# Placing the stages of a linear attention one by one between the MLP parts of the same kernel

## The chip, the cores and the metric

The kernel runs on one core of a Trainium2 chip. Such a core has engines that each work through their own list of instructions in order: TensorE (PE in the profile: matrix products, which read SBUF and write PSUM; its weight loads are shown as PEld), VectorE (DVE), ScalarE (ACT), GpSimd (POOL) and SyncE (SP, which here only issues DMAs). They wait for each other through semaphores. The metric is the time of one execution on the device in microseconds; the lower the better.

## The reference

The reference is a gated linear attention followed by an MLP with a residual.

```python
f = 1.0 / (1.0 + np.exp(-f_logit))              # (4, 8, 768, 48), as q, k and v
for t in range(S):
    state = f[:, :, t, :, None] * state + np.einsum('bhd,bhe->bhde', k[:, :, t], v[:, :, t])
    y[:, :, t] = np.einsum('bhd,bhde->bhe', q[:, :, t], state)
...
x = y.transpose(0, 2, 1, 3).reshape(4, 768, 384)
xn = (x - mu) / np.sqrt(var + 1e-06) * g_ln     # mean and variance of each row of 384
out = x + np.maximum(xn @ w_ch1, 0.0) @ w_ch2   # 384 x 1536 and 1536 x 384
```

The inputs of the attention are float32. The weights w_ch1 and w_ch2 arrive as 64-bit floating point numbers, and the kernel turns them into float32 on the chip.

## The kernel before, in words

**Units.** The sequence is cut into twelve units of 64 steps. A unit holds these 64 steps of all four batches and eight heads, that is 256 rows for the MLP, in two groups g of 128 rows. Only a state of 48 x 48 for each batch and head goes from one unit to the next.

**The attention of a unit** (attention(n), lines 494 to 624) is a generator with four stages, each ended by a yield:

1. TensorE transposes f (line 505), ScalarE makes the gates with a sigmoid (533), and VectorE runs two scans along the time: after (518), the product of the gates from a step to the end of the unit, and upto (527), the other way round, started from the reciprocal of the whole product (523, 525). least (538) keeps the smallest whole product, for a check at the end.
2. k and q are transposed, and VectorE multiplies them with the scans into kh and qh (546).
3. VectorE decays the state into kept (553). TensorE multiplies qh with kept into py (563) and kh with qh into the scores ps (573). VectorE masks them (576). kh is transposed back (584) and copied by ScalarE (586).
4. TensorE adds the scores times v to py (593). ScalarE copies py to x (604). VectorE takes the statistics of x (606, 607), GpSimd makes the reciprocal standard deviation (608, 609). TensorE forms the new part of the state (616), VectorE adds it (621; in unit 0 it copies it, 623).

Then normalize(n) (631, VectorE) and turn(n) (641 on TensorE, 643 on ScalarE) give xt, the operand of the MLP.

**The MLP of a unit** (mlp(n), lines 647 to 671) is a generator with twelve parts. Parts 0 to 5 form the first product, 256 of the 1536 columns each (656: twelve matmuls, as each float32 product is two instructions), with a ReLU on ScalarE (658). Parts 6 to 11 form the second product for the two groups (663, eight matmuls each). After parts 8 and 11 VectorE adds x (668), and SP writes the rows out (670).

**The weights.** w1 and w2 are cut into six pieces each (pieces, 428 to 433). A piece of w1 is what one of the parts 0 to 5 reads; a piece of w2 serves two steps of a group's sum of twelve. fetch() issues the DMA of a piece's words. split() (450 to 470) takes exponent and mantissa apart on VectorE (461, 463), converts both on ScalarE (465, 466), and lets GpSimd clamp and shift the exponent (468). join() (472 to 481) puts mantissa, sign and exponent together on VectorE (477, 479, 481).

**The order** is written by hand: each engine gets its instructions in the order in which the program emits them. After the first two units' attention and MLPs, whose order carries the weight conversion along (675 to 706), the loop of line 719 runs MLP m part by part, and between the parts the attention of unit m + 1: stage 1 after part 0, stage 2 after part 1, stage 3 after part 5, stage 4 after part 7, normalize after part 9, turn after part 10, and the loads of unit m + 2 after part 2. Unit 2's attention lies in the loop of line 709, between the second products of units 0 and 1.

**Buffers.** PSUM has eight banks. Four single banks (ps1, one_bank) serve, in turn, the transposes, parts 0 to 5, and one per group of the second product; two pairs of banks (ps2, two_banks) serve py, ps and the state. The transposed k and q take two single banks each, until kh and qh are formed. f, k and q have two buffers in SBUF, v three, the words of the weights three, and their exponents and mantissas two each.

Of the kernel before, what the change touches and what calls it, by code (L numbers as in the profile page):

```python
# [303 lines left out]
def kernel(  # L304
# [21 lines left out]
    P = 128  # L326
# [51 lines left out]
    def load(n, engines):  # L378
        if n >= NU:
            return  # L380
        vt = raws.tile([P, G, H, D], FP32, tag="rawv", name=f"v{n}")
        tiles = [wide_heads[name, n % 2] for name in "fkq"] + [vt]
        loaded[n] = tiles
        for t, src in zip(tiles, (f_logit, k, q, v), strict=True):
            for b in range(B):
                engines[b % len(engines)].dma_start(
                    out=t[(b % 2) * T:(b % 2 + 1) * T, b // 2, :, 0:D],
                    in_=src[b, :, n * T:(n + 1) * T, :].rearrange("h p d -> p h d"))

    load(0, (nc.sync, nc.scalar))  # L390
# [10 lines left out]
    power = consts.tile([P, 2], FP32)  # L401
    nc.vector.memset(power, -0.5)
    bias = consts.tile([P, 1], FP32)
    nc.vector.memset(bias, float(-BIAS))

    warm = consts.tile([P, 1], FP32)
    nc.scalar.activation(out=warm, in_=power[:, 0:1], func=AF.Sigmoid)
# [15 lines left out]

    load(1, (nc.sync,))
    nc.sync.dma_start(out=gain, in_=moe_g_ln.rearrange("(c p) -> p c", p=P))
# [24 lines left out]
    def split():  # L450

        if not fetched:
            return
        name, words, to, r, w = fetched.pop(0)
        scale = stage.tile([P, r, w], I32, tag="scale", bufs=2, name=f"{name}scale")
        frac = stage.tile([P, r, w], FP32, tag="frac", bufs=2, name=f"{name}frac")
        wv = words.rearrange("p r (f two) -> p two r f", two=2)
        low, high = wv[:, 0].bitcast(U32), wv[:, 1]


        nc.vector.tensor_scalar(out=scale, in0=high, scalar1=20, scalar2=0x7FF,
                                op0=ALU.logical_shift_right, op1=ALU.bitwise_and)
        nc.vector.tensor_scalar(out=frac.bitcast(I32), in0=high, scalar1=0xFFFFF, scalar2=None,
                                op0=ALU.bitwise_and)
        nc.scalar.activation(out=scale, in_=scale, func=AF.Relu, bias=bias, scale=1.0)  # L465
        nc.scalar.activation(out=frac, in_=frac.bitcast(I32), func=AF.Copy, bias=1.0,
                             scale=2.0 ** -20)
        nc.gpsimd.tensor_scalar(out=scale, in0=scale, scalar1=255.0, scalar2=float(1 << 23),  # L468
                                op0=ALU.min, op1=ALU.mult)
        opened.append((low, high, scale, frac, to))  # L470
# [23 lines left out]
    def attention(n):  # L494

        fr, kr, qr, vt = loaded.pop(n)
# [17 lines left out]
        def scans(s0, s1):  # L514
            c0, c1 = s0 * E1, s1 * E1
            flat = "p s e -> p (s e)"

            nc.vector.tensor_tensor_scan(  # L518
                out=after.rearrange(flat)[:, c0:c1][:, ::-1],
                data0=gt[:, c0 + 1:c1 + 1][:, ::-1],  # L520
                data1=ends.rearrange(flat)[:, c0:c1][:, ::-1], initial=0.0,
                op0=ALU.mult, op1=ALU.add)
            nc.vector.tensor_scalar_max(out=total[:, s0:s1], in0=after[:, s0:s1, 0],
                                        scalar1=1e-30)
            nc.vector.reciprocal(out=st[:, s0:s1, 0], in_=total[:, s0:s1])

            nc.vector.tensor_tensor_scan(  # L527
                out=upto.rearrange(flat)[:, c0:c1], data0=gt[:, c0:c1],
                data1=st.rearrange(flat)[:, c0:c1], initial=0.0, op0=ALU.mult, op1=ALU.add)

        for g in range(G):
            pt = across(fr, g)
            nc.scalar.activation(out=gv[:, g * HS:(g + 1) * HS, 1:E1], in_=pt, func=AF.Sigmoid)  # L533
            if n == 0:
                scans(g * HS, (g + 1) * HS)
# [12 lines left out]
        yield  # L548


        if n:
            kept = work.tile([P, 2, GA, D], FP32, tag="kept", name=f"kept{n}")
            nc.vector.tensor_tensor(
                out=kept, in0=state, op=ALU.mult,
                in1=total.rearrange("p (e b) -> p b e", b=2).unsqueeze(3).broadcast_to(
                    [P, 2, GA, D]))

# [11 lines left out]
        for e in range(GA):  # L569
            for b in range(2):  # L570
                for r in range(2):
                    seg = 2 * e + b
                    nc.tensor.matmul(ps[half(b), r, e], lhsT=kh[head_rows(r), seg],  # L573
                                     rhs=qh[head_rows(r), seg], start=True, stop=True)
        sc = work.tile([P, 2, GA, T], FP32, tag="sc", name=f"sc{n}")
        nc.vector.tensor_tensor(  # L576
            out=sc.rearrange("s r e t -> s (r e) t"), in0=ps.rearrange("s r e t -> s (r e) t"),
            in1=causal.unsqueeze(1).broadcast_to([P, 2 * GA, T]), op=ALU.mult)
        kt = work.tile([P, GA, P], FP32, tag="kt", name=f"kt{n}")
# [7 lines left out]
        yield  # L587
# [15 lines left out]
        for g in range(G):  # L603
            nc.scalar.copy(out=x[:, g].rearrange("t (a r d) -> t r a d", r=2, d=D),  # L604
                           in_=pyv[:, g])
            nc.vector.bn_stats(out=stats[:, g], in_=x[:, g])  # L606
# [3 lines left out]
        norm_of[n] = mv, rstd  # L610
        if n < NU - 1:
# [10 lines left out]
            else:  # L622
                nc.vector.tensor_copy(out=state, in_=pnv)
        yield
# [48 lines left out]


    for _ in range(3):
        fetch()
    first, second = attention(0), attention(1)
    for stages in (first, first, first, second, first, second):
        next(stages)
    normalize(0)  # L680
    turn(0)
    split()
    next(second)
    split()
    join()
    fetch()
    mlps = mlp(0), None
    for part in range(6):
        next(mlps[0])
        if part == 0:  # L690
            next(second)
        elif part == 1:
            normalize(1)
        elif part == 2:
            turn(1)
        split()
        join()
        fetch()
    mlps = mlps[0], mlp(1)
    for part in range(6):  # L700
        next(mlps[1])
        split()
        join()
        fetch()
        if part == 3:
            load(2, (nc.sync,))
    assert not (queue or fetched or opened)
    third = attention(2)
    for part in range(12):
        next(mlps[part // 6])  # L710
        if part in (1, 2, 5, 7):
            next(third)
        elif part == 3:
            load(3, (nc.sync,))
        elif part == 9:
            normalize(2)
        elif part == 10:
            turn(2)
    for m in range(2, NU):
        n = m + 1  # L720
        stages = attention(n) if n < NU else iter(())
        parts = mlp(m)
        for slot in range(12):
            next(parts)
            if slot in (0, 1, 5, 7):
                next(stages, None)
            elif slot == 2:
                load(n + 1, (nc.sync,))
            elif slot == 9 and n < NU:
                normalize(n)  # L730
            elif slot == 10 and n < NU:
                turn(n)
            if n == NU and slot == 2:
# [46 lines left out]
```

## Time and profile before

| what | value |
| --- | --- |
| time, median of three runs | 586.15 us (585.65 to 586.56) |
| time of the profiled execution | 586.91 us |
| its span, from the first to the last instruction | 585.2 us |
| mean granted TensorE clock | 0.947 of full speed |
| TensorE busy | 518.4 us (89%) |
| VectorE busy | 217.5 us (37%) |
| ScalarE busy | 118.4 us (20%) |
| GpSimd busy | 52.9 us (9%) |

The profile shows one execution. Busy times are sums of an engine's instructions. A group of instructions is given as line, engine, operation, output <- inputs, shapes, count, busy time, mean ns of one, and the idle time just before it with what ended it. In a row of the timeline the first number is the start in us and the second the length. In a row of the chain it is the same, without the engine's waits. A row of the windows gives the stretch, its length, then the busy time and the number of instructions of TensorE, its weight loads, VectorE, ScalarE and GpSimd, then the granted clock, the share of the DMA engines, and GB/s.

### The profile page before, as it was taken

To read this page: it belongs to the slowest core of one execution; us is meant where nothing else is said; L and a number is where in the kernel's file an instruction comes from. 1 tells how busy PE (TensorE), PEld (TensorE's weight loads), DVE (VectorE), ACT (ScalarE), POOL (GpSimd) and SP (SyncE) were. 2 spreads that over 40 slices of the span, in tenths; PEclk is the share of its full clock that TensorE was granted. 3 is DMA by queue.
4 is the path that set the end of the run, shared out by engine and by line. 5 is a ranking of instruction groups with operands and counts; after the bars stand their busy time and mean duration, and the time that the engine had idled before them with its cause. 6 is when DMAs were issued, how large, how long until landed. Compare 5 with 4: busy or idle time off the path is not lost.

```text
span 585.2 us, 10892 instructions
## 1 busy us (share of the span) xinstructions
PE 518.4 (89%) x4841; PEld 396.7 (68%) x4841; DVE 217.5 (37%) x312; ACT 118.4 (20%) x242; POOL 52.9 (9%) x53
## 2 busy tenths in 40 slices
PE   4645779789899899989989989989989989989996
PEld 3644558456686686777777777777777777777773
DVE  4774878922412323323232233232232242252000
ACT  1242435200211211211211211211211211211110
POOL 3024448200000000000000000000000000000000
PEclk9957779989989989989989999989989989999999
DMA  9901535760420320330330330330340240100101
GB/s 141 232 7 55 162 115 168 95 136 16 76 47 15 73 50 10 72 56 2 69 67 2 62 73 3 70 65 3 60 76 2 52 85 2 28 0 2 27 4 31
DMA packets 109703, 33.83 MB, mean 58 GB/s; under 512 B 102736, under 2 KB 105808, under 8 KB 109648
## 3 DMA queue, kind: packets, MB, share of 16 engines
q1 hardware_dynamic: 105424, 32.26, 26.8%
q10 hardware_dynamic: 4224, 0.79, 1.1%
q8 instruction: 40, 0.66, 0.5%
q14 instruction: 15, 0.12, 0.1%
HBM read 28.31 MB, written 4.72 MB: 56 GB/s over the span
## 4 chain that ended last, share of the span: by engine, by line
PE 72%; DVE 19%; ACT 3%; issue 1%; POOL 1%; DMA 1%; DVEq 0%; ACTq 0%
PE po L663 31%; PE ph L656 28%; DVE upto L527 5%; DVE after L518 5%; PE py L593 4%; PE ps L573 2%; PE py L563 2%; PE kp L584 2%; ACT gates L533 2%; DVE w L481 2%; PE pn L616 2%; PE xp L641 1%; DVE kh L546 1%; DVE w_0scale L479 1%; DMA qraw<-in_q_dram 1%
## 5 line engine op out<-in xcount | busy, mean ns | idle before, releaser
L656 PE MATMUL ph<-xt,w 128*128 128x256 f32 x864 | 213.2, 408 | 38.0 <-DVE kh L546 21.1
L656 PEld LDWEIGHTS ph<-xt,w 128*128 128x128 f32 x864 | 176.1, 206 | 70.8 <-DVE kh L546 23.2
L663 PE MATMUL po<-w,h 128*128 128x384 f32 x576 | 194.5, 492 | 0.6 <-DVE w L481 0.6
L663 PEld LDWEIGHTS po<-w,h 128*128 128x128 f32 x576 | 107.7, 191 | 70.0 <-issue 1.5
L658 ACT ACTIVATE h<-ph 128x512 f32<-128x512 f32 x72 | 42.9, 597 | 215.1 <-PE ph L656 215.1
L576 DVE TENSOR_TENSOR sc<-ps,causal 128x1024 f32<-128x1024 f32 x12 | 14.7, 1225 | 110.4 <-PE ps L573 110.4
L668 DVE TENSOR_TENSOR o<-x,po 128x384 f32<-128x384 f32 x24 | 13.3, 554 | 109.9 <-PE po L663 109.9
L608 POOL TENSOR_SCALAR rstd<-mv 128x2 f32<-128x2 f32 x12 | 2.7, 223 | 455.3 <-DVE mv L607 455.3
L606 DVE BATCH_NORM_STATS2 stats<-x 128x6 f32<-128x384 f32 x24 | 13.0, 543 | 81.8 <-ACT x L604 81.8
L518 DVE TENSOR_TENSOR_SCAN after<-gates,ends 128x1040 f32<-128x1040 f32 (+1 forms) x13 | 28.0, 2156 | 41.0 <-ACT gates L533 41.0
L643 ACT ACTIVATE xt<-xp,gain 128x128 f32<-128x128 f32 x72 | 19.9, 376 | 91.6 <-PE xp L641 91.6
L527 DVE TENSOR_TENSOR_SCAN upto<-gates,starts 128x1040 f32<-128x1040 f32 (+1 forms) x13 | 28.1, 2158 | 0.4
L593 PEld LDWEIGHTS py<-v,sc 64*64 64x64 f32 x768 | 23.3, 135 | 5.9 <-issue 5.9
L593 PE MATMUL py<-v,sc 64*64 64x48 f32 x768 | 24.8, 219 | 0.0
L604 ACT COPY x<-py 128x384 f32<-128x384 f32 x24 | 10.3, 482 | 67.5 <-PE py L593 67.5
L586 ACT COPY kt<-kp 128x512 f32<-128x512 f32 x24 | 13.1, 588 | 53.7 <-PE kp L584 53.7
L468 POOL TENSOR_SCALAR w_0scale<-w_0scale 128x768 int32<-128x768 int32 x7 | 22.2, 3171 | 14.7 <-ACT w_0scale L465 14.7
L573 PE MATMUL ps<-qh,kh 48*64 48x64 f32 x768 | 15.2, 235 | 5.7 <-DVE qh L546 5.7
L573 PEld LDWEIGHTS ps<-qh,kh 48*64 48x64 f32 x768 | 14.0, 149 | 6.2 <-DVE qh L546 6.2
L505 PE MATMUL tr<-ident,fraw 128*128 128x128 f32 x96 | 13.6, 285 | 5.1 <-DMA fraw<-in_f_logit_dram 5.1
L505 PE MATMUL tr<-ident,qraw 128*128 128x128 f32 x96 | 13.6, 286 | 3.6 <-DVE o L668 2.8
L505 PEld LDWEIGHTS tr<-ident,fraw 128*128 128x128 f32 x96 | 11.8, 148 | 6.7 <-POOL causal L398 4.4
(95 smaller groups left out, 328.8 us busy)
## 6 DMA issues: line engine op xcount, KB each, us to landing
w_0words<-in_moe_w_ch_dram SPq DMA_DIRECT2D x7, 768.0 KB, 4.3
out_dram<-o SPq DMA_DIRECT2D x48, 96.0 KB, 2.2
fraw<-in_f_logit_dram SPq DMA_DIRECT2D x46, 96.0 KB, 3.0
kraw<-in_k_dram SPq DMA_DIRECT2D x46, 96.0 KB, 3.2
qraw<-in_q_dram SPq DMA_DIRECT2D x46, 96.0 KB, 3.0
v<-in_v_dram SPq DMA_DIRECT2D x46, 96.0 KB, 3.2
w_256words<-in_moe_w_ch_dram SPq DMA_DIRECT2D x1, 768.0 KB, 6.2
w_512words<-in_moe_w_ch_dram SPq DMA_DIRECT2D x1, 768.0 KB, 8.7
```

What stands on the lines that cost most here:

```text
L468: nc.gpsimd.tensor_scalar(out=scale, in0=scale, scalar1=255.0, scalar2=float(1 << 23), op0=ALU.min, op1=ALU.mult)
L505: nc.tensor.transpose(pt[:, a * P:(a + 1) * P], src[:, g, 2 * a:2 * a + 2].rearrange("p h e -> p (h e)"), ident)
L518: nc.vector.tensor_tensor_scan(out=after.rearrange(flat)[:, c0:c1][:, ::-1], data0=gt[:, c0 + 1:c1 + 1][:, ::-1], data1=ends.rearrange(fla ...
L527: nc.vector.tensor_tensor_scan(out=upto.rearrange(flat)[:, c0:c1], data0=gt[:, c0:c1], data1=st.rearrange(flat)[:, c0:c1], initial=0.0, op ...
L573: nc.tensor.matmul(ps[half(b), r, e], lhsT=kh[head_rows(r), seg], rhs=qh[head_rows(r), seg], start=True, stop=True)
L576: nc.vector.tensor_tensor(out=sc.rearrange("s r e t -> s (r e) t"), in0=ps.rearrange("s r e t -> s (r e) t"), in1=causal.unsqueeze(1).broa ...
L593: nc.tensor.matmul(py[half(b), r, e * D:(e + 1) * D], lhsT=sc[half(b), r, e], rhs=vt[half(b), g, 2 * a + r], start=n == 0 and e == 0, stop ...
L643: nc.scalar.mul(out=xt[:, m, g * P:(g + 1) * P], in_=pt[:, m], mul=gain[:, m:m + 1])
L656: nc.tensor.matmul(ph[:, j], lhsT=w1[:, m, (i + j) * P:(i + j + 1) * P], rhs=xt[:, m], start=m == 0, stop=m == KD - 1)
L658: nc.scalar.activation(out=h[:, i:i + 2], in_=ph, func=AF.Relu)
L663: nc.tensor.matmul(po, lhsT=h[:, i, g * P:(g + 1) * P], rhs=w2[:, i], start=i == 0, stop=i == KF - 1)
L668: nc.vector.tensor_tensor(out=o, in0=x[:, g], in1=po, op=ALU.add)
```

## The change

The generator of the attention now has named stages: gates, after, upto, k, q, scores, causal, kt, values, stats, state, norm and turn follow one another (norm and turn, the former normalize and turn, are called from it), and each place names the stages that it runs. In the loop over the later units, gates and after follow part 0, upto part 1, k part 2, q (with least and kept) part 3, scores, causal and kt part 5, values, stats and state part 7, norm part 9, turn part 10; the loads go from behind part 2 to behind part 3. Unit 2's attention is spread likewise.

In the first two units w1 is converted between unit 0's stages and the first parts of its MLP, before unit 1's scans; w2's pieces come in unit 1's attention and in the first parts of its MLP. join() comes ahead of split() of the next piece. The loads of unit 0 leave ScalarE's queue except two of f, the first two weight pieces are fetched ahead of unit 1's loads, and ScalarE's first sigmoid comes before k, q and v are issued. GpSimd's clamp and shift becomes two instructions on ScalarE, and unit 0's state is copied by ScalarE.

```diff
-    def load(n, engines):
+    def load(n, name, engines=(nc.sync,)):
...
-    load(0, (nc.sync, nc.scalar))
+    load(0, "f", (nc.sync, nc.scalar))
+
+    power = consts.tile([P, 2], FP32)
+    nc.vector.memset(power, -0.5)
+    warm = consts.tile([P, 1], FP32)
+    nc.scalar.activation(out=warm, in_=power[:, 0:1], func=AF.Sigmoid)
+    for name in "kqv":
+        load(0, name)
...
+    full = consts.tile([P, 1], FP32)
+    nc.vector.memset(full, 255.0)
...
-    load(1, (nc.sync,))
-    nc.sync.dma_start(out=gain, in_=moe_g_ln.rearrange("(c p) -> p c", p=P))
...
-        nc.scalar.activation(out=scale, in_=scale, func=AF.Relu, bias=bias, scale=1.0)
         nc.scalar.activation(out=frac, in_=frac.bitcast(I32), func=AF.Copy, bias=1.0,
                              scale=2.0 ** -20)
-        nc.gpsimd.tensor_scalar(out=scale, in0=scale, scalar1=255.0, scalar2=float(1 << 23),
-                                op0=ALU.min, op1=ALU.mult)
+        nc.scalar.activation(out=scale, in_=scale, func=AF.Relu, bias=bias, scale=1.0)
+        nc.scalar.activation(out=scale, in_=scale, func=AF.Relu, bias=full, scale=-1.0)
+        nc.scalar.activation(out=scale, in_=scale, func=AF.Copy, bias=float(255 << 23),
+                             scale=float(-(1 << 23)))
...
+        yield "gates"
         if n:
-            scans(0, NS)
-        nc.vector.tensor_tensor(out=least, in0=least, in1=total, op=ALU.min)
-        yield
+            scan_after(slice(0, NS))
+        yield "after"
+        if n:
+            scan_upto(slice(0, NS))
+        yield "upto"
...
-        yield
+            if dst is kh:
+                yield "k"
+        nc.vector.tensor_tensor(out=least, in0=least, in1=total, op=ALU.min)
...
-                nc.vector.tensor_copy(out=state, in_=pnv)
-        yield
+                nc.scalar.copy(out=state, in_=pnv)
+        yield "state"
+        normalize(n)
+        yield "norm"
+        turn(n)
+        yield "turn"
...
+    fetch()
+    fetch()
+    load(1, "f")
+    nc.sync.dma_start(out=gain, in_=moe_g_ln.rearrange("(c p) -> p c", p=P))
+    fetch()
+    for name in "kqv":
+        load(1, name)
+
+    def weights(*steps):
+        for step in steps:
+            step()
+            if step is join:
+                fetch()
+
+    do.attention(0, "gates", "after", "upto", "k", "q", "scores")
+    weights(split)
+    do.attention(0, "causal", "kt", "values")
+    weights(join, split)
+    do.attention(0, "stats", "state")
+    do.attention(1, "gates")
+    weights(join, split)
+    do.attention(0, "norm", "turn")
+    do.mlp(0)
+    weights(join, split)
+    do.mlp(0)
     for _ in range(3):
...
+        weights(join, split)
+        do.mlp(0)
+    do.attention(1, "after", "upto", "k", "q")
+    weights(join)
+    do.mlp(0)
+    do.attention(1, "scores")
+    weights(split)
+    do.attention(1, "causal", "kt", "values")
+    weights(join, split)
+    do.attention(1, "stats", "state")
+    weights(join)
+    do.attention(1, "norm", "turn")
     for part in range(6):
...
+        do.mlp(1)
+        weights(split, join)
+        if part == 3:
+            for name in "fkqv":
+                load(2, name)
...
     for part in range(12):
...
+        do.mlp(part // 6)
+        if part == 1:
+            do.attention(2, "gates", "after")
         elif part == 2:
...
+            do.attention(2, "upto")
+            for name in "fkqv":
+                load(3, name)
         elif part == 3:
...
+            do.attention(2, "k")
+        elif part == 4:
+            do.attention(2, "q")
+        elif part == 6:
+            do.attention(2, "scores", "causal", "kt")
+        elif part == 8:
+            do.attention(2, "values", "stats", "state")
...
     for m in range(2, NU):
         n = m + 1
...
+        for part in range(12):
+            do.mlp(m)
+            if part == 0:
+                do.attention(n, "gates", "after")
+            elif part == 1:
+                do.attention(n, "upto")
+            elif part == 2:
+                do.attention(n, "k")
+            elif part == 3:
+                do.attention(n, "q")
+                for name in "fkqv":
+                    load(n + 1, name)
+            elif part == 5:
+                do.attention(n, "scores", "causal", "kt")
+            elif part == 7:
+                do.attention(n, "values", "stats", "state")
+            elif part == 9:
+                do.attention(n, "norm")
+            elif part == 10:
+                do.attention(n, "turn")
```

Here do.attention(n, ...) advances the generator of unit n by the named stages, and do.mlp(n) runs the next part of MLP n.

More of the change, by code (lines that the diff above doesn't have):

```diff
@@ L715 @@
         elif part == 9:
[L716 removed]
+            do.attention(2, "norm")
         elif part == 10:
[L718 removed]
+            do.attention(2, "turn")
     for m in range(2, NU):
         n = m + 1
[L721 to L733, printed above, removed]
+        for part in range(12):
+            do.mlp(m)
[17 more added lines that the diff above has]
+                do.attention(n, "turn")
+            if n == NU and part == 2:
```

104 lines of the change are left out of this document (47 added, 57 removed).

## The prediction

> **What bounds the kernel now.** I read the page first: busy shares, the chain that ended last, the costliest groups.
>
> ```profile
> span 585.2 us, 10892 instructions
> ...
> PE 72%; DVE 19%; ACT 3%; issue 1%; POOL 1%; DMA 1%; DVEq 0%; ACTq 0%
> ...
> L656 PE MATMUL ph<-xt,w 128*128 128x256 f32 x864 | 213.2, 408 | 38.0 <-DVE kh L546 21.1
> ```
>
> The chain is TensorE for 72% and VectorE for 19%. The first matmuls of the MLP are the only large group with idle time before them, 38.0 us. The view of waits says whom they waited for (us in total, times, longest):
>
> ```profile
> PE ph L656 <- DVE kh L546: 21.1, 9, 2.4
> ...
> PE ph L656 <- DVE w L481: 16.9, 4, 6.2
> ```
>
> So there are two places. Nine times, once in each unit's MLP from unit 2 to unit 10, TensorE waits for the product kh of the attention next to it. Four times, in the first unit's MLP, it waits for a converted piece of w1. One of the nine, in the timeline:
>
> ```profile
> 243.35 2.76 PE L656 MATMUL ph<-xt,w 128*128 128x256 f32 x12
> 244.28 2.33 DVE L518 TENSOR_TENSOR_SCAN after<-gates,ends 128x1040 f32<-128x1040 f32 x1 [3.64 <-ACT gates L533]
> ...
> 247.14 2.33 DVE L527 TENSOR_TENSOR_SCAN upto<-gates,starts 128x1040 f32<-128x1040 f32 x1
> ...
> 249.45 1.28 DVE L546 TENSOR_TENSOR kh<-tr,after 128x512 f32<-128x512 f32 x2
> ...
> 250.19 12.31 PE L656 MATMUL ph<-xt,w 128*128 128x256 f32 x48 [2.34 <-DVE kh L546]
> ...
> 251.84 0.95 DVE L553 TENSOR_TENSOR kept<-state,total 128x768 f32<-128x768 f32 x1
> ```
>
> Part 1 of the MLP (243.35, twelve matmuls) is followed on TensorE at once by the sixteen transposes of k and q. They fill the four single PSUM banks, and part 2 wants one of these. A bank comes free only when VectorE has done both scans and the first kh product. That is 2.34 us of standing still, and it costs more than itself. In the chain in order of time the next 48 matmuls have these lengths (nine such rows in all: two of 10.63, seven of 12.20 to 12.31):
>
> ```profile
> 160.65 12.31 PE ph L656 x48
> ...
> 294.96 12.20 PE ph L656 x48
> ...
> 339.63 10.63 PE ph L656 x48
> ...
> 517.01 10.63 PE ph L656 x48
> ```
>
> The view by windows has the reason (the number behind the busy times is the granted clock):
>
> ```profile
> 250.20:254.80 4.60, 4.60 (x14) 3.77 (x15) 2.60 (x4) 0.03 (x1) 0.00 (x0) 0.63 0.73 137
> 254.80:262.50 7.70, 7.70 (x40) 6.52 (x40) 0.00 (x0) 1.76 (x3) 0.00 (x0) 1.00 0.01 2
> 339.60:350.20 10.60, 10.57 (x51) 9.06 (x51) 2.63 (x4) 1.79 (x3) 0.00 (x0) 1.00 0.36 68
> ```
>
> After seven of the nine stalls the clock is low for about the first 4.6 us (0.63), after two it stays at 1.00. A lowered clock costs 12.31 - 10.63 = 1.68 us.
>
> **The change part by part. First, the steady loop.** Scan after stays behind part 0; upto goes behind part 1, the k transposes and kh behind part 2, q and kept behind part 3, the scores remain behind part 5. I lay this out from the unit above. VectorE runs after and upto from 244.28 to 249.47 as before, since nothing else is queued there. TensorE goes from part 1 straight to part 2; a part is 2.60 us in the chain (row at 150.45 below), so part 1 ends at 245.95 and the k transposes come at 248.6. The kh product follows upto without a gap, 249.5 to 250.7. TensorE does part 3 from about 249.4 to 252.0, then q, and qh and kept end near 255.0. Parts 4 and 5 end at 258.1, where the scores need kept: 3 us to spare. At most one pair of transposes holds banks at a time, and part 3 takes the third or fourth. So I see nothing late next, and the stall goes: 9 x 2.34 = **21.1 us**, as the view of waits totals it. If the cover were gone, the scores would wait for kept by what VectorE is late beyond 3 us.
>
> The clock loss goes with the stall: six times 1.68 and once 1.57, **11.6 us**. From below it is 0, if the dips have another cause.
>
> The Trainium skill, "TensorE: Matmul & The Clock Gate", Part 1, has the clock fall to half after at least one idle window of about 3.4 us. By that alone a 2.34 us stall could not lower it, and the 11.6 us would not come from it; the sum would be 562. The trace speaks against this reading: 0.63 follows the stall and nothing else. The same page, Part 4, says that transposes do not count as busy time the same way; counted with the sixteen transposes, the stretch without ordinary matmuls is 245.95 to 250.19, 4.24 us.
>
> Moving the loads behind part 3 costs nothing: between the two places no other instruction stands on SP's queue, so its order is the same. The smallest value of the gate products, least, moves behind qh on VectorE, in the 3 us to spare; it is read only after the last unit.
>
> **The start.** Each weight piece is opened by two VectorE instructions, finished by three, with ScalarE and so far GpSimd in between. From the groups by line, shapes kept apart (behind the first bar: busy us, mean ns of one):
>
> ```profile
> L658 ACT ACTIVATE h<-ph 128x512 f32<-128x512 f32 x72 | 42.9, 597 | 215.1 <-PE ph L656 215.1
> ...
> L468 POOL TENSOR_SCALAR w_0scale<-w_0scale 128x768 int32<-128x768 int32 x7 | 22.2, 3171 | 14.7 <-ACT w_0scale L465 14.7
> ...
> L479 DVE SCALAR_TENSOR_TENSOR w_0scale<-w_0words,w_0scale 128x768 int32<-128x768 int32 x7 | 8.6, 1224 | 1.2 <-POOL w_0scale L468 1.2
> ...
> L477 DVE SCALAR_TENSOR_TENSOR w_0frac<-w_0words,w_0frac 128x768 f32<-128x768 uint32 x7 | 6.7, 954 | 1.4 <-ACT w_0frac L466 1.4
> L465 ACT ACTIVATE w_0scale<-w_0scale,bias 128x768 int32<-128x768 int32 x7 | 6.6, 937 | 6.5 <-DVE w_0scale L461 6.5
> L466 ACT ACTIVATE w_0frac<-w_0frac 128x768 f32<-128x768 int32 x7 | 5.9, 838 | 0.1
> ...
> L461 DVE TENSOR_SCALAR w_0scale<-w_0words 128x768 int32<-128x768 int32 x7 | 3.9, 559 | 0.2
> ...
> L481 DVE TENSOR_TENSOR w<-w_1024frac,w_1024scale 128x768 f32<-128x768 f32 x1 | 1.0, 959 | 0.0
> ...
> L479 DVE SCALAR_TENSOR_TENSOR w_1024scale<-w_1024words,w_1024scale 128x768 int32<-128x768 int32 x1 | 1.0, 958 | 0.2 <-POOL w_1024scale L468 0.2
> ```
>
> GpSimd's 3.17 us is replaced by a Relu with a bias tile and a Copy on ScalarE. The trace has neither on this tile in this place; the nearest rows are L465 (0.94) and L466 (0.84) with the same shape and type, and L468 itself as the upper end (3.17 each); the lower end is that both hide. I take 0.94 + 0.84. With GpSimd out of it, L479 should stay at 0.96 instead of its mean of 1.22. One piece in turn is then: L461 and its like 1.05, ScalarE 0.84 + 0.94 + 0.94 + 0.84 = 3.55, L479 and L481 1.95 (L477 lies beside ScalarE), hand-overs 0.15: **6.7 us a round**. The new order gives join of one piece and then split of the next, so rounds do not overlap: each split waits behind a join, and each join for ScalarE. That is the price of this order. Queued behind a piece on ScalarE stand ReLUs, kt and the copies of x; they come up to 3.55 us later, and who waits for them (the statistics, unit 1's turn) is in the sum below.
>
> For the start of the rounds, the timeline:
>
> ```profile
> 3.60 1.87 POOL L415 MEMSET gates<- 128x1041 f32 x2
> ...
> 8.32 1.28 ACT L407 ACT_TABLE_LOAD   x1 [8.32 <-DMA qraw<-in_q_dram]
> ...
> 10.33 1.24 DVE L518 TENSOR_TENSOR_SCAN after<-gates,ends 128x520 f32<-128x520 f32 x1 [5.93 <-ACT gates L533]
> ...
> 14.80 2.67 SPq L386 DMA_DIRECT2D qraw<-in_q_dram  x4
> ...
> 17.33 1.28 DVE L546 TENSOR_TENSOR qh<-tr,upto 128x512 f32<-128x512 f32 x2
> ...
> 20.90 1.25 SPq L447 DMA_DIRECT2D w_0words<-in_moe_w_ch_dram  x1
> ...
> 33.35 0.86 DVE L631 TENSOR_SCALAR xn<-x,mv,rstd 128x384 f32<-128x384 f32 x2
> ...
> 34.88 1.66 ACT L643 ACTIVATE xt<-xp,gain 128x128 f32<-128x128 f32 x6 [9.21 <-PE xp L641]
> ```
>
> ScalarE's table load waited until 8.32 behind its own DMA issues. With two left there the gates can start when GpSimd's fill ends (5.5), the scans at about 6.1 instead of 10.33, and qh is done near 14.5. SP now issues the k, q and v of unit 0 alone: with two for f that is fourteen issues at 0.67 us (a quarter of 2.67), and the first words go out near 10.5 instead of 20.90, ahead of unit 1's loads. So the first round starts at about 15.2. From there: rounds 0 to 2, 20.1, to 35.3, where the first unit's part 0 can run. It runs at low clock (4.53, row at 82.62 below), and its ReLU of 0.6 stands ahead of piece 3 on ScalarE: 40.4. Piece 3 from there 3.55 + 1.95 = 45.9, pieces 4 and 5 two rounds, 59.3, split of the next 60.3. Only then come the scans of unit 1: from after to the end of kept 8.5 (244.28 to 252.79 above), 68.8; join of w2's first piece 2.9, 71.7; two more pieces, each opened, waited for and joined at 6.7, 85.1; then xn to the end of xt 3.2 (33.35 to 36.54). The second unit's part 0 would start at **88.3**. Against before (chain in order of time):
>
> ```profile
> 82.62 4.53 PE ph L656 x12
> ...
> 150.45 2.60 PE ph L656 x12
> ...
> 326.25 0.66 PE xp L641 x6
> 326.90 2.58 PE po L663 x8
> ...
> 369.33 0.66 PE xp L641 x6
> ```
>
> There it followed at 87.15, with the first unit's last part. So w1 ahead of the chain gains nothing by itself: what TensorE waits less for w1 (16.9) it waits for unit 1's turn. Behind it lies 150.45 - 87.15 = 63.3 us until unit 2's part 0. A whole unit at full clock is 369.33 - 326.25 - 2.34 = 40.74; this stretch has six parts of the second product more (2.58 each, 15.5) and 1.9 for a cold first part. About 1.0 comes from ScalarE: w2's last three pieces run in rounds from 93.4, its last instruction ends near 110.2, and three ReLUs and unit 2's gates (0.6 each, same shape) follow until 113, while TensorE asks for a bank at 112. That is 59.1. Unit 2's part 0 starts at 147.4, **3.0 us** earlier. The bounds here are (b) and (c) below. Unit 0's state goes from VectorE to ScalarE (near L466's 0.84); only unit 1's kept at 68 reads it, so it is hidden.
>
> **Sum.** 21.1 + 11.6 + 3.0 = 35.7. The profiled execution took 586.91 (span 585.2, 1.7 around it), 0.76 over the median 586.15. 586.15 - 35.7 = **550.5 us**.
>
> **The rivals.** (a) The clock keeps dipping for a reason other than the stall: 550.5 + 11.6 = 562.1. For it speaks that two of nine stalls had no dip, against it that no dip comes without one in the steady part. (b) The start is dearer, a round of 8 us in place of 6.7, or ReLUs that hold banks behind the conversion on ScalarE: eight rounds x 1.3 = 10.4, 561. (c) The start is cheaper, because TensorE's cold parts and the scans hide more: a round of 5.7 gives 543. (d) The stall stays, in another part, since a bank is still held by something that waits for VectorE: only the start changes, 583.2. The layout above speaks against it. (e) Slower than before: the two new ScalarE instructions run on integers at GpSimd's 3.17 each. That is 4.6 us more a round, on eight rounds before the second unit and three in its MLP: 11 x 4.6 = 51, 601. It turns to the slow side from 35.7 / 11 = 3.2 us a round, at 2.5 us an instruction. L465 and L466, 0.94 and 0.84 on integers, speak against it.
>
> **How the numbers follow.** Forecast 0.62 (545 to 557), (a) 0.07, (b) 0.12, (c) 0.12, (d) 0.04, (e) 0.03. The range 541 to 563 takes in the forecast, (a), (b) and most of (c). A measurement of this kernel tells 0.2% (1.2 us) from no change. Faster 0.95, within 0.2% 0.02, slower 0.03.
>
> **What would show it.** The wait of ph for kh gone from the view of waits, the distance from one xp to the next near 40.7 in every unit, the granted clock at 1.00 from unit 2 on; the second unit's part 0 near 88 and unit 2's near 147.4; the new ScalarE instructions at 0.84 to 0.94, L479 near 0.96. I am wrong if a wait for kept or for a bank takes the stall's place, or if a round is far from 6.7.

## The result and the profile after

| | before | after |
| --- | --- | --- |
| median of four runs | 586.33 us (585.65 to 586.56) | 546.46 us (545.63 to 546.86) |
| the profiled execution: span | 585.2 us | 543.9 us |
| unit 2's part 0 begins | 150.45 us | 143.82 us |
| from there to the end of the span | 434.75 us | 400.08 us |
| TensorE, VectorE, ScalarE, GpSimd busy | 518.4, 217.5, 118.4, 52.9 us | 500.2, 212.1, 140.0, 16.4 us |

The ratio is 0.932 (95% interval 0.9304 to 0.9336). The gain of 39.9 us was forecast as 35.7. Of the 41.3 us between the two spans, 34.7 lie in the loop and 6.6 before it.

The page of the kernel after, with its chain, its slices and its costliest group:

```profile
span 543.9 us, 10888 instructions
...
PEclk9969787999999999999999999999999999999999
...
PE 84%; DVE 6%; ACT 5%; SPq 2%; DMA 1%; issue 1%
...
L681 PE MATMUL ph<-xt,w 128*128 128x256 f32 x864 | 200.9, 389 | 7.8 <-DVE w L485 4.6
```

TensorE now holds 84% of the chain where it had 72%, and VectorE 6% where it had 19%. The idle time before the first product fell from 38.0 to 7.8 us. Its busy time fell as well, from 213.2 to 200.9, although it is the same 864 matmuls. Most of these 12.3 us is what the low clock had cost (11.6 by the prediction's nine rows): PEclk stays at 9 from the eighth slice on, and a window over unit 2's MLP, 143.82 to 184.31, gives a granted clock of 1.00.

The longer waits of TensorE after:

```profile
PE xp L666 <- DVE xn L656: 14.4, 2, 7.2
...
PE tr L509 <- DVE kh L559: 7.2, 1, 7.2
...
PE ph L681 <- DVE w L485: 4.6, 2, 3.7
```

The nine waits of ph for kh are gone, and no wait of TensorE that is left happens more than twice, so none belongs to the loop. The wait of ph for w fell from 16.9 to 4.6. In its place xp waits 14.4 for xn (before: one wait of 6.4), and once a transpose waits 7.2 for kh. So in the start a part of the wait has moved to unit 1's turn.

The chain of the kernel after in order of time (start, length, what; waits left out):

```profile
82.28 0.96 DVE w L485
83.24 0.40 DVE xn L656
...
85.82 17.58 PE ph L681 x72
...
143.82 2.59 PE ph L681 x12
146.41 0.87 PE tr L509 x8
147.28 5.18 PE ph L681 x24
152.47 0.87 PE tr L509 x8
153.34 2.59 PE ph L681 x12
...
181.07 0.66 PE xp L666 x6
...
221.55 0.65 PE xp L666 x6
```

From 143.82 on each row begins where the one before ended: part 0, the transposes of f, parts 1 and 2, the eight transposes of k, part 3. No row of VectorE stands between them. The distance from one xp to the next is 40.48 us (221.55 - 181.07); before it was 43.08 in a unit without a dip of the clock (a stretch in which the granted clock is low), and 1.7 more in one with it. The first two rows show what stands behind "xp waits for xn": xn's turn came when the join of w2's third piece (L485) had ended. The view of waits names the last instruction, the chain names the queue ahead of it.

### The profile page after: what moved, and what is told of

Same layout as the page of the kernel before. It is cut to its first block, busy times and chain, and to the rows that moved or that the text cites. A ratio compares the mean times of both kernels' runs of the same rounds, so it can differ in the third digit from the quotient of the medians.

```text
span 543.9 us, 10888 instructions
## 1 busy us (share of the span) xinstructions
PE 500.2 (92%) x4841; PEld 384.9 (71%) x4841; DVE 212.1 (39%) x312; ACT 140.0 (26%) x267; POOL 16.4 (3%) x41
## 4 chain that ended last, share of the span: by engine, by line
PE 84%; DVE 6%; ACT 5%; SPq 2%; DMA 1%; issue 1%
PE po L688 35%; PE ph L681 33%; PE tr L509 5%; PE py L611 4%; PE py L579 2%; PE kp L602 2%; PE ps L589 2%; SPq L388 2%; PE pn L637 2%; DVE w L485 1%; PE xp L666 1%; DMA w_0words<-in_moe_w_ch_dram 1%; DVE w_0scale L483 1%; ACT w_0scale L471 1%; ACT w_0scale L472 0%
## 5 line engine op out<-in xcount | busy, mean ns | idle before, releaser
L681 PE MATMUL ph<-xt,w 128*128 128x256 f32 x864 | 200.9, 389 | 7.8 <-DVE w L485 4.6
L681 PEld LDWEIGHTS ph<-xt,w 128*128 128x128 f32 x864 | 166.7, 196 | 34.2 <-issue 4.1
L666 PE MATMUL xp<-ident,xn 128*128 128x128 f32 x72 | 11.2, 298 | 14.4 <-DVE xn L656 14.4
L559 DVE TENSOR_TENSOR qh<-tr,upto 128x512 f32<-128x512 f32 x24 | 15.5, 686 | 19.6 <-PE tr L509 19.6
L666 PEld LDWEIGHTS xp<-ident,xn 128*128 128x128 f32 x72 | 9.5, 154 | 17.9 <-issue 9.2
L509 PEld LDWEIGHTS tr<-ident,qraw 128*128 128x128 f32 x96 | 12.0, 150 | 9.6 <-DVE kh L559 7.4
```

The source lines that it names most:

```text
L509: nc.tensor.transpose(pt[:, a * P:(a + 1) * P], src[:, g, 2 * a:2 * a + 2].rearrange("p h e -> p (h e)"), ident)
L559: nc.vector.tensor_tensor(out=dst[:, segs], in0=pt, in1=by[:, segs, 1:E1], op=ALU.mult)
L666: nc.tensor.transpose(pt[:, m], xn[:, g, m * P:(m + 1) * P], ident)
L681: nc.tensor.matmul(ph[:, j], lhsT=w1[:, m, (i + j) * P:(i + j + 1) * P], rhs=xt[:, m], start=m == 0, stop=m == KD - 1)
```

## The experiments

The ratio of each is to runs of the kernel before on the same chip. "Unit 2's part 0" is the row like the one at 143.82 above.

**Half of the change at a time.** loop_only is the kernel before with only the loop's stages spread (and so unit 2's):

```diff
-        yield
+            if dst is kh:
+                yield
...
-            if slot in (0, 1, 5, 7):
+            if slot in (0, 1, 2, 3, 5, 7):
```

> The kernel before with the stages of units 2 to 11 placed one by one as after the change, the first two units untouched. Theory (the gain sits in the loop: nine stalls and the clock they cost): the distance from one xp to the next falls to 40.5 in every unit, the granted clock stays at 1.00 from unit 2 on, and the time is 586.3 - 34.7 = 551.6. Rival (the gain comes from the start, which lets everything follow earlier): above 575.

It took 552.32 us against 587.60, ratio 0.9399 (0.937 to 0.9428): 35.3 us less. Its chain has the new distance in every unit:

```profile
147.69 0.66 PE xp L651 x6
188.17 0.66 PE xp L651 x6
```

start_only is the changed kernel with the loop's old places:

```diff
-                do.attention(n, "gates", "after")
+                do.attention(n, "gates", "after", "upto")
             elif part == 1:
-                do.attention(n, "upto")
+                do.attention(n, "k", "q")
```

> The changed kernel with the old placement in the loop for units 3 to 11 (gates, after and upto behind part 0, k and q behind part 1); the start and unit 2 as changed. Theory: the nine stalls of 2.3 to 2.4 us are back, with seven to nine dips of the clock, and only the 6.6 us of the start remain: 579.7, 576 to 583 by the number of dips. Rival: under 565.

581.89 us, ratio 0.9881 (0.9841 to 0.9922): 5.7 us less. Its chain shows the old loop again, with eight long rows and one short (two of the nine here):

```profile
334.19 12.21 PE ph L681 x48
...
378.78 10.63 PE ph L681 x48
```

35.3 + 5.7 = 41.0 against 39.9 for both: the parts add up within what the runs scatter, and the loop is six sevenths of the gain.

**Is it the bank?** If a stall comes from q's transposes holding the bank that part 2 wants, another place for them should end it with every stage left in its old place. q_in_pair puts q's transposes of each group into one half of a pair of banks:

```diff
+            pair = two_banks(f"trq{n}") if n > 2 and dst is qh else None
             for g in range(G):
-                pt = across(src, g)
+                if pair is None:
+                    pt = across(src, g)
+                else:
+                    for a in range(NP):
+                        nc.tensor.transpose(pair[:, g, a * P:(a + 1) * P], ...)
+                    pt = pair[:, g].rearrange("p (s t) -> p s t", t=T)
```

> The kernel before, its order of stages unchanged, with one edit: from unit 3 on the transposes of q go into one of the two pairs of PSUM banks instead of two single banks. Theory (the stall is a want of a single PSUM bank): with two single banks more the stall goes without moving any stage, unit distance 40.5, about 552. Rival (the matmuls wait for the scans by the order of the stages, whatever the banks): stall and time as before, 586.

607.70 us, ratio 1.0354 (1.0307 to 1.0402). It went to the slow side, which neither theory had expected. Its waits and its timeline:

```profile
PE trq L549 <- DVE qh L554: 35.8, 9, 4.0
```

```profile
249.53 0.60 PE L549 MATMUL trq<-ident,qraw 128*128 128x128 f32 x4
...
253.36 0.69 DVE L554 TENSOR_TENSOR qh<-trq,upto 128x512 f32<-128x512 f32 x1
254.10 1.11 PE L549 MATMUL trq<-ident,qraw 128*128 128x128 f32 x4 [3.97 <-DVE qh L554]
```

The second group's four transposes wait for the first group's product, though they write the other half. Both halves are one tile, and here the program's order puts the write of the second half behind the read of the first. So the stall of 2.34 became one of 3.97 ahead of part 2, nine times.

q_pair_whole mends this: the transposes of both groups go into the pair before either product.

```diff
+            if n > 2 and dst is qh:
+                pair = two_banks(f"trq{n}")
+                for g in range(G):
+                    for a in range(NP):
+                        nc.tensor.transpose(pair[:, g, a * P:(a + 1) * P], ...)
```

> As q_in_pair, but both groups' transposes of q are issued before either product reads the pair, so that no transpose waits for a product of the same tile. Theory (want of a single PSUM bank): the stall goes, unit distance 40.5, about 552. Rival (the order of the stages): stall and time as before, 586.

553.29 us, ratio 0.9417 (0.9375 to 0.9459), the gain of loop_only. Its timeline, with kh behind both scans as before:

```profile
238.81 1.04 PE L547 MATMUL trq<-ident,qraw 128*128 128x128 f32 x8
...
239.69 10.53 PE L666 MATMUL ph<-xt,w 128*128 128x256 f32 x48
241.45 1.28 DVE L556 TENSOR_TENSOR kh<-tr,after 128x512 f32<-128x512 f32 x2
```

Parts 2 to 5 (239.69) start before kh (241.45), without a wait. What held TensorE was the bank and nothing of the attention's data. The spread of stages is one way to have a bank free, a pair of banks is another.

**Is the clock the stall's?** The next three kernels keep the old loop and give TensorE work in the stall, behind the sixteen transposes. It is added work whose result is not used. fill_matmuls adds five float32 products of 128x256 (ten instructions), fill_two two of them, and fill_transposes twenty transposes:

```diff
+            if slot == 1 and n < NU:
+                fill = two_banks(f"fill{n}")
+                for _ in range(5):
+                    nc.tensor.matmul(fill[:, 0, 0:2 * P], lhsT=w1[:, 0, 0:P],
+                                     rhs=w1[:, 0, 0:2 * P], start=True, stop=True)
```

> The kernel before with five products of constant operands (128x256, never read; 2.2 us of TensorE at full clock) put into the stall of units 3 to 11; part 2 waits for VectorE as before. It adds work and leaves none out. Theory (the clock falls because TensorE stands still): all nine units keep the clock at 1.00, 48 matmuls take 10.63, unit distance 43.1, time 586.3 - 11.7 = 574.6. Rival (the dip has another cause): 12.31 stays in seven units, 586 or, since the filling may run over, somewhat more.

> As fill_matmuls, but the stall is filled with twenty transposes of constant operands (128x128, 2.2 us at 0.109 each). Theory (transposes do not count as activity for the clock): the dips stay, in seven to nine units, 583 to 589. Rival (any work on TensorE counts): no dip, 574.6 as with filled-in products.

> As fill_matmuls with two products in place of five: 0.9 us of the stall filled, some 1.5 us left. If the clock falls by how much of a stretch stands idle, the dips get fewer or vanish: 574.6 to 580. If any halt of TensorE between the transposes and part 2 lowers it, seven or more stay: 583 to 587.

| kernel | us | ratio | longest stall left | long rows of 48 matmuls |
| --- | --- | --- | --- | --- |
| fill_matmuls | 576.46 | 0.9802 (0.9776 to 0.9828) | 0.2 us | 0 of 9 |
| fill_transposes | 575.83 | 0.9818 (0.9789 to 0.9847) | 0.2 us | 0 of 9 |
| fill_two | 576.21 | 0.9814 (0.9769 to 0.9858) | 1.5 us | 0 of 9 |

Against the runs before on the same chip, added work made the kernel faster by 11.1, 10.6 and 10.6 us. The timelines of fill_transposes and then of fill_two at the same stall:

```profile
243.13 1.04 PE L505 MATMUL tr<-ident,kraw 128*128 128x128 f32 x8
244.00 1.04 PE L505 MATMUL tr<-ident,qraw 128*128 128x128 f32 x8
244.88 2.35 PE L730 MATMUL fill<-ident,w 128*128 128x128 f32 x20
247.38 3.94 PE L656 MATMUL ph<-xt,w 128*128 128x256 f32 x17 [0.15 <-DVE kh L546]
```

```profile
244.67 1.03 PE L730 MATMUL fill<-w 128*128 128x256 f32 x4
247.17 4.15 PE L656 MATMUL ph<-xt,w 128*128 128x256 f32 x18 [1.47 <-DVE kh L546]
```

and two of the nine rows of 48 matmuls in the chain of fill_transposes:

```profile
204.29 10.63 PE ph L656 x48
...
247.38 10.63 PE ph L656 x48
```

In fill_transposes TensorE does nothing but transposes from 243.13 to 247.38, 4.25 us, and the row behind is 10.63 each time. So here a transpose kept the clock up as a product did. In fill_two TensorE stands still for 1.47 us, and the clock stays as well. What lowered it was a stand-still of 2.3 to 2.4 us by the view of waits, in seven of nine cases before and eight of nine in start_only.

Why the others escaped can be read from windows that are cut where the clock changes. Three stalls of the kernel before: the dip behind the stall at 247.85, then the window that holds most of the next stall and the one behind it, with a dip, and the same two windows for the last stall, which had none.

```profile
250.40:253.82 3.42, 3.42 (x9) 2.71 (x9) 2.40 (x4) 0.00 (x0) 0.00 (x0) 0.50 0.79 149
...
291.37:294.78 3.41, 1.25 (x12) 1.02 (x10) 3.31 (x6) 0.15 (x1) 0.00 (x0) 1.00 0.81 147
294.78:298.19 3.41, 3.23 (x8) 2.60 (x9) 2.79 (x5) 0.00 (x0) 0.00 (x0) 0.50 0.78 148
...
513.23:516.64 3.41, 1.44 (x14) 1.20 (x12) 3.31 (x6) 0.33 (x1) 0.00 (x0) 1.00 0.00 0
516.64:520.05 3.41, 3.04 (x14) 2.71 (x15) 2.97 (x5) 0.15 (x1) 0.00 (x0) 1.00 0.00 0
```

A dip is one stretch of 3.41 us at half the clock, and the dips lie on a grid of this step: from 250.40 to 294.78 it is 44.38 us, thirteen steps. Ahead of the second dip TensorE stood still for 2.16 us within one stretch (3.41 - 1.25). Ahead of 516.64 it was 1.97 (3.41 - 1.44), since an edge of the grid cuts that stall; the clock stayed. The other stall without a dip is cut likewise, with 1.86 in one stretch (335.73 to 339.15). The same split holds in start_only (2.08 or more ahead of each dip, 1.87 without one) and in q_in_pair (2.05 or more with a dip, at most 1.92 without one), and the stall of fill_two is too short for it. So for these stalls the bound lies between 1.97 and 2.05 us within one stretch, and whether a stall of 2.3 us lowers the clock depends on where it falls on the grid. For other work it is not shown: at the start of chain_gpsimd a stretch with 1.67 us of standing still went low as well. By the same count the 4.25 us of transposes, at least 2.1 of them in one stretch, would have lowered the clock nine times had they counted as standing still.

**The start.** gpsimd_back is the changed kernel with GpSimd's clamp and shift instead of the two ScalarE instructions. With it comes the old order on ScalarE, the exponent's Relu ahead of the mantissa's Copy:

```diff
+        nc.scalar.activation(out=scale, in_=scale, func=AF.Relu, bias=bias, scale=1.0)
         nc.scalar.activation(out=frac, in_=frac.bitcast(I32), func=AF.Copy, bias=1.0,
                              scale=2.0 ** -20)
-        nc.scalar.activation(out=scale, in_=scale, func=AF.Relu, bias=bias, scale=1.0)
-        nc.scalar.activation(out=scale, in_=scale, func=AF.Relu, bias=full, scale=-1.0)
-        nc.scalar.activation(out=scale, in_=scale, func=AF.Copy, ...)
+        nc.gpsimd.tensor_scalar(out=scale, in0=scale, scalar1=255.0, scalar2=float(1 << 23),
+                                op0=ALU.min, op1=ALU.mult)
```

> The changed kernel with GpSimd's clamp and shift back in place of the two ScalarE instructions. Theory (ScalarE makes the round shorter, also because GpSimd slows VectorE beside it): a round of about 7.4 in place of 6.5, second unit's part 0 some 7 us later than 85.8, about 553. Rival (ScalarE is the scarce engine at the start, and two instructions less per piece let kt, the copies and the ReLUs come earlier): 546 or less.

544.05 us, ratio 0.9269 (0.9245 to 0.9293): 2.4 us faster than the changed kernel, and the two intervals don't meet. One round in the timeline of the changed kernel, and then in that of gpsimd_back:

```profile
45.06 0.55 DVE L464 TENSOR_SCALAR w_1024scale<-w_1024words 128x768 int32<-128x768 int32 x1
...
46.12 0.84 ACT L468 ACTIVATE w_1024frac<-w_1024frac 128x768 f32<-128x768 int32 x1 [2.47 <-DVE w_1024frac L466]
...
47.82 0.93 ACT L471 ACTIVATE w_1024scale<-w_1024scale,full 128x768 int32<-128x768 int32 x1
48.79 0.84 ACT L472 ACTIVATE w_1024scale<-w_1024scale 128x768 int32<-128x768 int32 x1
...
49.66 0.96 DVE L483 SCALAR_TENSOR_TENSOR w_1024scale<-w_1024words,w_1024scale 128x768 int32<-128x768 int32 x1 [1.70 <-ACT w_1024scale L472]
...
51.53 0.55 DVE L464 TENSOR_SCALAR w_1280scale<-w_1280words 128x768 int32<-128x768 int32 x1
```

```profile
43.34 0.55 DVE L464 TENSOR_SCALAR w_1024scale<-w_1024words 128x768 int32<-128x768 int32 x1
...
43.93 0.94 ACT L468 ACTIVATE w_1024scale<-w_1024scale,bias 128x768 int32<-128x768 int32 x1 [3.58 <-DVE w_1024scale L464]
...
44.94 2.77 POOL L471 TENSOR_SCALAR w_1024scale<-w_1024scale 128x768 int32<-128x768 int32 x1 [3.51 <-ACT w_1024scale L468]
...
45.63 0.96 DVE L480 SCALAR_TENSOR_TENSOR w_1024frac<-w_1024words,w_1024frac 128x768 f32<-128x768 uint32 x1 [1.26 <-ACT w_1024frac L469]
...
47.75 0.96 DVE L482 SCALAR_TENSOR_TENSOR w_1024scale<-w_1024words,w_1024scale 128x768 int32<-128x768 int32 x1 [1.16 <-POOL w_1024scale L471]
...
49.62 0.55 DVE L464 TENSOR_SCALAR w_1280scale<-w_1280words 128x768 int32<-128x768 int32 x1
```

The round is 51.53 - 45.06 = 6.47 us with ScalarE and 49.62 - 43.34 = 6.28 with GpSimd. From ScalarE's first instruction to L483 or L482 it is 3.54 us with ScalarE alone (46.12 to 49.66) and 3.82 with GpSimd (43.93 to 47.75), so that part is no shorter with GpSimd. But in the changed kernel the mantissa's Copy comes first and begins 1.06 us behind L464; in gpsimd_back the exponent's Relu comes first and begins 0.59 behind it. So the rows put the gain down to the order of these two, which the edit changes along with the engine. A kernel with ScalarE alone and the exponent first was not run; by these rows its round would be about 6.0 us (an estimate, 6.47 - 0.47). Since join precedes split, VectorE has only L480 to do while GpSimd works; it takes 0.96 there, and L482, which follows, 0.96 too.

split_first lets the next piece be opened before the last is joined, everywhere in the start:

```diff
-    weights(join, split)
+    weights(split, join)
```

> The changed kernel with split of the next piece ahead of join of the last one in every place where both stand together. Theory (the serial round of 6.5 us is what the start costs): ScalarE works on a piece while VectorE joins the one before, rounds of about 4.5, the second unit's part 0 near 77 in place of 85.8, about 537. Rival (the start is bound by something else, so a shorter round only makes other waits longer): 546.

536.41 us, ratio 0.9143 (0.9119 to 0.9167). Its timeline:

```profile
38.82 0.56 DVE L464 TENSOR_SCALAR w_1024scale<-w_1024words 128x768 int32<-128x768 int32 x1
...
42.69 0.56 DVE L464 TENSOR_SCALAR w_1280scale<-w_1280words 128x768 int32<-128x768 int32 x1
```

A round is 3.87 instead of 6.47. Unit 2's part 0 comes at 134.65, 9.2 earlier than in the changed kernel, which is less than eight times the 2.6 saved in a round. In the view of waits one piece now waits for its words:

```profile
DVE w_768scale L464 <- DMA w_768words<-in_moe_w_ch_dram: 5.9, 1, 5.9
```

chain_in_waits goes on from there and puts unit 1's stages one by one between the first unit's parts and the pieces. chain_join_first is the same with the changed kernel's join and split order, and chain_gpsimd the same as chain_in_waits with GpSimd:

```diff
     do.attention(0, "norm", "turn")
+    weights(split, join)
+    do.attention(1, "after")
     do.mlp(0)
-    weights(join, split)
+    weights(split, join)
+    do.attention(1, "upto")
     do.mlp(0)
...
-    do.attention(1, "after", "upto", "k", "q")
```

> As split_first, and unit 1's stages stand between the first unit's MLP parts and the pieces (after ahead of part 0, upto ahead of part 1, k behind it, and so on), so that its scans run while VectorE waits for ScalarE; w1 is no longer converted ahead of unit 1's chain. Theory (the second unit's chain is what comes late, and VectorE has idle time for it): second unit's part 0 near 66 to 70, unit 2's near 122 to 126, time 524 to 530. Rival (w1 ahead of the chain is the better order): not under split_first, 537 or more.

> As chain_in_waits, but with join ahead of split again in each place: unit 1's stages in the waits, rounds not overlapped. Theory (two separate gains): second unit's part 0 near 74, unit 2's near 138, about 541, so that the placement of unit 1's chain is worth some 6 us alone and the overlapped rounds the rest. Rival (the placement does it all): 526 as chain_in_waits.

> As chain_in_waits with GpSimd's clamp and shift in place of the two ScalarE instructions. Theory (GpSimd and VectorE slow each other when they run side by side, which the overlapped order makes them do): slower than chain_in_waits, 529 to 535. Rival (ScalarE's relief counts for more, as in the non-overlapped order): 522 to 525.

| kernel | us | ratio | second unit's part 0 | unit 2's part 0 |
| --- | --- | --- | --- | --- |
| changed kernel | 546.46 | 0.932 (0.9304 to 0.9336) | 85.82 | 143.82 |
| split_first | 536.41 | 0.9143 (0.9119 to 0.9167) | 76.16 | 134.65 |
| chain_join_first | 534.43 | 0.9099 (0.9058 to 0.914) | 71.52 | 132.77 |
| chain_in_waits | 526.31 | 0.8969 (0.8947 to 0.8992) | 66.61 | 122.85 |
| chain_gpsimd | 528.58 | 0.8991 (0.895 to 0.9033) | 69.98 | 127.90 |

By the medians the place of unit 1's stages alone is worth some 12.0 us, the order of split and join alone 10.1, both together 20.2 (the kernel before took 586.3 to 586.8 on the chips of these runs). I had put the first at about 6. chain_in_waits beats both kernels of the study: 60 us under the one before, 20 under the changed one.

In chain_gpsimd GpSimd and VectorE work at the same time. Its groups by line:

```profile
L471 POOL TENSOR_SCALAR w_0scale<-w_0scale 128x768 int32<-128x768 int32 x7 | 22.7, 3248 | 25.0 <-ACT w_0scale L468 24.9
...
L482 DVE SCALAR_TENSOR_TENSOR w_0scale<-w_0words,w_0scale 128x768 int32<-128x768 int32 x7 | 7.9, 1134 | 0.7 <-POOL w_0scale L471 0.7
```

and two rows of its timeline:

```profile
36.22 2.92 POOL L471 TENSOR_SCALAR w_768scale<-w_768scale 128x768 int32<-128x768 int32 x1 [2.68 <-ACT w_768scale L468]
36.44 1.57 DVE L482 SCALAR_TENSOR_TENSOR w_512scale<-w_512words,w_512scale 128x768 int32<-128x768 int32 x1
```

GpSimd's mean is 3.25 us where it was 2.77 in gpsimd_back, and L482's mean is 1.13 instead of 0.96; where L482 begins just behind a GpSimd instruction, as in these two rows, it takes 1.57. So ScalarE in GpSimd's place may pay where rounds overlap, but the times do not show it: the medians are 2.3 us apart and the intervals of the two ratios overlap. The 5.0 us between the profiled executions at unit 2's part 0 compare the fastest execution of chain_in_waits (524.47) with the slowest of chain_gpsimd (529.5).

## Why the prediction was right, and where its sizes were off

**The stall goes, and nothing takes its place: right.** loop_only shows it by itself. The prediction had the decayed state (the tile kept) ready 3 us before the scores' stage asks for it. In the unit behind 221.55 it ends at 239.61, and the first product that reads it, py, begins at 242.89: 3.3 us. The mechanism, a bank held until VectorE has done its scans and kh, is what q_pair_whole shows.

**Its size was 2.60 and not 2.34 a unit.** The term of 21.1 took the sum from the view of waits. Units without a dip went from 43.08 to 40.48, so nine times 2.60 is 23.4. The idle number starts at the recorded end of the last transposes, 246.81 + 1.04 = 247.85. But eight transposes take 0.87 of the chain when a product follows (146.41 to 147.28 above). The product could have begun at 247.68, 2.5 us before 250.19. The idle number leaves out this tail of the instruction ahead. The other 0.1 lies in the row behind: the 48 matmuls are recorded with 10.63 behind a stall and with 10.53 where they follow the transposes at once (q_pair_whole at 239.69).

**The clock goes with the stall, 11.6 us: right in size and cause, wrong in one of its explanations.** 23.4 + 11.6 = 35.0 against the 34.7 measured from unit 2's part 0 to the end, and rival (a) is out. The fill kernels show the cause: with the stall filled and nothing else changed, every long row went. The prediction read the dip as 0.63 for 4.6 us, which is the mean of a window that ends too late; it is 0.50 for 3.41 us, with the same loss of 1.7. But the prediction offered the Trainium skill, "TensorE: Matmul & The Clock Gate", Part 4, as a bridge: transposes might not count as busy, which would make the idle stretch 4.24 us. fill_transposes has such a stretch of 4.25 us, nine times, and no dip. Here the transposes counted. The window of about 3.4 us in Part 1 of that page of the Trainium skill is found in the trace as the stretch of 3.41 us; but it did not have to be idle as a whole, 2.05 us within it was enough.

**The start gave 6.6 us and not 3.0.** The 3.6 us between have four main parts. Part 0 of the first unit was put behind the third join, at 35.3; it does not read that piece and began at 34.38. Piece 3 followed its ReLU, and the next L464 came at 45.06 and not at 45.9, 0.8. The round was forecast at 6.7 and measured at 6.47: the first three make up for a first L464 that came at 15.78 and not at 15.2, the two ahead of unit 1's scans and the two behind kept give 0.9. From xn to part 0 it took 2.6 and not 3.2, 0.6 more; with 0.1 from the join behind kept that makes 85.82 where 88.3 was forecast. The stretch behind it was 58.0 and not 59.1, as the 1.0 that I had charged for late ReLUs isn't to be found in the view of waits. Within the round the instructions were right (ScalarE's new ones 0.94 and 0.84, L483 at 0.96, so rival (e) is out). Too much was 0.15 for hand-overs, which the durations hold already, and 0.1 by which the next L464 begins ahead of L485's recorded end. Which of the start's own edits brought the 6.6 us is not taken apart: no run leaves out the moved loads or the earlier sigmoid alone.

**"w1 ahead of the chain gains nothing by itself"** agrees with the view of waits, though no run tests it by itself: ph waits 12.3 us less for w, xp 8.0 more for xn and a transpose 7.2 more for kh. chain_join_first shows the price of that order: with unit 1's stages in the waits for the pieces, some 12 us come back.

**"Rounds do not overlap, that is the price of this order"** is shown by split_first, 10.1 us. What a round would be with GpSimd in this order the prediction didn't work out; gpsimd_back has it at 0.2 us less. So the exchange together with the new order on ScalarE cost a little instead of saving; that the order is the cause is argued from the rows above and not shown by a run.

## What to carry to other kernels

When TensorE waits nine times for a product it does not read, look for the PSUM bank that the product frees; spreading the transposes or giving them other banks takes the wait away, and a stand-still of 2.3 us can cost 1.7 more through the clock. Price such a stall by the distance between units with and without it, not by the idle number. Where conversion and a dependent chain share VectorE and ScalarE, open the next piece before closing the last, and put the chain's stages into the waits: here that brought 20 us beyond the changed kernel, whose own start had brought 6.6.

## What the runs showed of the hardware that was not expected

- Twenty 128x128 float32 transposes in the stall kept the clock at full speed, as ten product instructions did: 10.63 us for the 48 matmuls behind in nine of nine cases.
- A stand-still of 1.5 us did not lower it (none of nine). One of 2.3 to 2.4 us did in seven of nine and eight of nine. The clock then stood at 0.50 for one stretch of 3.41 us, on a grid of the same step; ahead of each dip of the loop at least 2.05 us of standing still lay in one stretch, in the cases that escaped at most 1.97.
- GpSimd's clamp and shift of 128x768 integers took 2.77 us with only L480 of VectorE beside it and 3.25 in the mean of chain_gpsimd. VectorE's L482 went from 0.96 to 1.57 where it began 0.2 us behind a GpSimd instruction; L480, 0.7 us behind one, stayed at 0.96.
